# A spectral filter beside a gated feed-forward block on one core: the first three gated units split by row tile, the first loads reordered, two down projections put side by side, one pair of returns issued earlier

## The chip, the core and the metric

The kernel runs on one core of a Trainium2 chip. The metric is device time in microseconds (us) of one execution. The engines are named as in the profile: PE (TensorE matmul), PEld (its weight loads), DVE (VectorE), ACT (ScalarE), POOL (GpSimd) and SP (SyncE, which here only issues DMAs). ACT issues a few DMAs too; its issues are shown as ACTq, those of SP as SPq. Every engine works through its own list of instructions in order.

## The reference

For x of 2048 rows by 512 columns, with xn = layernorm(x) by row:

```python
def _A_ref(x, w_r, w_i):            # spectral filter
    X = rfft2(x.astype(float32)) * (w_r + 1j * w_i)     # 2048 x 257
    return irfft2(X, s=(S, D)).astype(bfloat16)

def _B_ref(x, w_gate, w_up, w_down):                    # 512 -> 1792 -> 512
    g = einsum("bsd,df->bsf", x, w_gate)
    u = einsum("bsd,df->bsf", x, w_up)
    return einsum("bsf,fd->bsd", gelu_tanh(g) * u, w_down)

out = x + _A_ref(xn, A_w_r, A_w_i) + _B_ref(xn, B_w_gate, B_w_up, B_w_down)
```

All inputs and the output are bf16.

## The kernel before

The rows form 16 tiles of 128 (x_sb, numbered j) and four blocks of four tiles (numbered b). The 1792 inner columns form 14 groups of 128 (numbered fc).

**Gated half.** A gated unit (`geglu_unit`, PE at L543) is one block and one group fc: four matmuls with the gate weights, four with the up weights, each for up to 512 rows, then a gelu on ACT (L555) and a product on DVE (L563) into hT. The gate and the up product take one PSUM bank each out of a ring, and the ring hands a bank out again only when ACT or DVE has read it. When a block's 14 units are done, four down units (`down_unit`, 14 matmuls at L589) project its hT by w_down, one per row tile, and DVE adds the result to x_sb (L600). The down units of blocks 0 to 2 have a ring of one bank, bank 7 (`ring_dn`); those of block 3 take the three banks of the gated units.

**Spectral half.** The Fourier transforms are chains of small matmuls: per row tile unit A (L616) and unit d (L642), a shuffle through device memory (`stage_p` out by SP, back into Tp by `shuffle`), per pair of frequency groups unit B (L691), the filter's product on DVE (L708 to L710) and unit c (L722), a second trip through device memory (`stage_g` out by SP, back into V by `back`, L739), and per row tile unit e (L753) and unit fin (L774), whose last steps run on ACT, DVE and POOL and add to x_sb. `back` is issued in four parts of two DMAs. Unit e of any tile waits for all eight (`perm2`).

**Order.** The program is one list per engine, written by hand (`_Sched`). Each entry carries the events that it waits for. Gated and down units serve as fillers between the spectral units: a list `fillers` holds the units of the four blocks in order, with the down units of block b-1 inserted among the gated units of block b at given places, and `filler(n)` takes the next n. One filler stands in each step of the A/d loop (16 steps), in steps 1 to 17 of the B/c loop (19 steps, numbered u), and in most steps of the e/fin loop. Between the B/c loop and the e/fin loop stand `todo["left"] - 15 - 3` fillers, five of them. For block 3 the insert places are (3, 5, 7, 14), so the five are the last gated unit of block 2, three gated units of block 3, and one down unit of block 2.

**Head.** SP issues the first loads, one stream (semaphore) for each x tile and one for each weight piece, gate and up together. DVE takes the row statistics (L411, L412), ACT the square root of the first two tiles (L417), DVE the reciprocal (L421) and the normalised rows (L434). For tiles 2 and 3 POOL computes the reciprocal root (L426, L427). In the meantime PE runs 46 and then 4 matmuls on zeros (`warm_up`, L524). Then PE transposes tiles 0 and 1 (`transposes_by_tile`, L447) into four banks, DVE and ACT copy them to xnT (L453, L455), and the first six gated units (`NHALF = 6`) run on rows 0 to 255 of block 0, then on rows 256 to 511, with a ring of six banks (`ring_first`). The transposes of tiles 2 and 3 (L473) stand behind the fourth of these units. The other eight groups of block 0 come as fillers of 512 rows.

Of the kernel before, what the change touches and what calls it, by code (L numbers as in the profile page):

```python
# [14 lines left out]
HD = 256  # L15
# [6 lines left out]
NFC = 14  # L22
NGG = 3
NX1 = 4
NWARM = (46, 4)
LN_EPS = 1e-5


# [199 lines left out]
def bass_parallel_sum__spectral_gfnet__glu_gated_geglu__prompt_kernel(  # L228
# [21 lines left out]
    with ExitStack() as es:  # L250
# [68 lines left out]
        def sp_bank_bf(slot):  # L319
# [8 lines left out]
        ring_tr = _Ring((3, 4), bank_readers)  # L328

        streams = [("pe", 1), ("act", 1), ("dve", 1), ("pool", 1)]  # L330
        streams += [(n, 16) for n in ("x0", "x1", "x2", "x3", "xc1", "xc2", "xc3", "ident", "small", "fa", "eg", "wd", "wr", "wi",
                                      "w0", "w1", "w2", "w3", "w4", "dr0", "dr1", "perm1", "jx0", "jx1", "jx2", "jx3", "vd0_0", "vd0_1", "vd0_2", "vd1_0", "vd1_1", "vd1_2", "vd2_0", "vd2_1", "vd2_2", "vd3_0", "vd3_1", "vd3_2", "perm2", "tr2", "tr3", "out")]
# [15 lines left out]
        def load_w(i, which=(0, 1), eng="sp"):  # L348
            a, b = WPIECES[i]
            for q in which:  # L350
                dst, src = ((wg_sb, B_w_gate), (wu_sb, B_w_up))[q]
                load("w%d" % i, dst[:, :, a:b], src[:, a:b].rearrange("(r p) f -> p r f", p=P), eng=eng)
            ev_w[i] = total("w%d" % i)

        def load_xc(m):
            ev = load("xc%d" % m, x_sb[:, 4 * m:4 * m + 4, :], xv[:, 4 * m:4 * m + 4, :])
# [1 line left out]
                ev_x[j] = ev  # L358

        ev_x = {}  # L360
        load_w(0, (1,), eng="act")
        for j in range(4):
            ev_x[j] = load("x%d" % j, x_sb[:, j, :], xv[:, j, :])
            if j == 1:
                load_w(0, (0,))
        load_w(1)
        load_w(2)
        load_xc(1)
        load_w(3)
# [66 lines left out]

        ev_xnT = {}

        def transposes_by_tile(a, b, ring):

            n = (b - a) * P
            slots = [ring.alloc(1) for _ in range(NDC)]
            banks = [sp_bank_bf(slot)[:, 0:n] for slot, _ in slots]
            evs = []
            for j in range(a, b):
                for r in range(NDC):
                    ev_t = sch.op("pe", lambda e, j=j, r=r: e.transpose(banks[r][:, (j - a) * P:(j - a + 1) * P], xn[:, j, r * P:(r + 1) * P], ident),  # L447
                                  deps=[ev_id, ev_xn[j]] + slots[r][1])
                    if j < b - 1:
                        continue  # L450
                    dst = xnT[:, r, a * P:b * P]
                    if r % 2 == 0:
                        ev = sch.op("dve", lambda e, dst=dst, r=r: e.tensor_copy(dst, banks[r]), deps=[ev_t])  # L453
                    else:
                        ev = sch.op("act", lambda e, dst=dst, r=r: e.activation(dst, banks[r], ACT.Copy), deps=[ev_t])  # L455
                    ring.add_reader(slots[r][0], ev)
                    evs.append(ev)
            for j in range(a, b):
                ev_xnT[j] = evs

        def transposes(a, b, ring, per=2):

# [66 lines left out]
        def geglu_unit(b, fc, a=0, w=512, ring=None):  # L529

            k = geg["k"]
            geg["k"] = k + 1
            s2 = k % NGG
            hb = b % 2
            ring = ring or ring_gu
            evw = [ev_w[i] for i, (lo, hi) in enumerate(WPIECES) if lo < (fc + 1) * P and fc * P < hi]
            evx = [ev_xnT[4 * b + i] for i in range(a // P, (a + w) // P)]
            gslot, gdeps = ring.alloc(1)

            def mm(e, wsb, slot, dcs=range(NDC)):  # L540
                ins = None
                for dc in dcs:
                    ins = e.matmul(gu_bank(slot)[:, 0:w], wsb[:, dc, fc * P:(fc + 1) * P], xnT[:, dc, b * 512 + a:b * 512 + a + w],  # L543
                                   start=(dc == 0), stop=(dc == NDC - 1))
                return ins

            if b == 0 and fc == 0 and a == 0:
                for dc in range(NDC):
                    ev_gm = sch.op("pe", lambda e, dc=dc: mm(e, wg_sb, gslot, (dc,)), deps=evw + [x[dc] for x in evx] + gdeps)
            else:  # L550
                ev_gm = sch.op("pe", lambda e: mm(e, wg_sb, gslot), deps=evw + evx + gdeps)
            uslot, udeps = ring.alloc(1)
            ev_um = sch.op("pe", lambda e: mm(e, wu_sb, uslot), deps=udeps)
            gg = gg_sb[s2][:, 0:w]
            ev_gg = sch.op("act", lambda e: e.activation(gg, gu_bank(gslot)[:, 0:w], ACT.Gelu_apprx_tanh),  # L555
                           deps=[ev_gm] + gg_readers[s2])
# [238 lines left out]
            finished(j, ev_o)  # L795


        NHALF = 6
        ln_stats(0)
        ln_stats(1)  # L800
        ev_sq = ln_sqrt(0, 2)
        sch.op("act", lambda e: e.activation(warm[:], eps_t[:], ACT.Gelu_apprx_tanh), deps=[ev_eps])
        ln_recip(0, 2, ev_sq)
        for n, ev in zip(NWARM, (None, ev_rstd[0])):
            warm_up(n, ev)
        ln_apply(0)
        ln_apply(1)
        transposes_by_tile(0, 2, ring_sp)
        ln_stats(2)
        ln_stats(3)  # L810
        ln_rstd(2, 4)
        for fc in range(NHALF):
            geglu_unit(0, fc, 0, 256, ring_first)
            if fc == 1:
                ln_apply(2)
                ln_apply(3)
                half_fold(0)
            if fc == 3:
# [141 lines left out]
```

## Time and profile before

| | us |
|---|---|
| median of three runs (180.42 to 181.10) | 181.07 |
| the profiled execution's own time | 180.17 |
| its span, first to last instruction | 178.4 |
| PE busy | 174.7 (98%) |
| DVE busy | 116.0 (65%) |
| ACT busy | 86.5 (49%) |
| POOL busy | 55.2 (31%) |
| first gated matmul starts | 7.14 |
| first unit e starts | 128.63 |

The share of PE counts the time in which any matmul is in flight. A matmul of 128x512 shows 0.38 us, while the next starts 0.216 us after it; so a late start is found by comparing starts, not by idle time alone. The granted clock of the profile's row is full throughout. Yet the 50 zero matmuls of 128 columns at the head fill the time from 0.97 to 6.22, 0.105 us each, while the eight transposes right behind them, of the same size, show 0.61 us together. The DMA engines are busy from 2 us on up to about 53 us, with the loads of weights, x, constants and filter.

### The profile page before, as it was taken

The page shows a single profiled execution, that of the slowest core. Times are in us where ns is not written, and L with a number is a line of the kernel's source. Part 1 is how long each engine was busy: PE and PEld are TensorE (multiplying, and loading weights), DVE is VectorE, ACT ScalarE, POOL GpSimd, SP SyncE. Part 2 cuts the span into 40 slices and gives each one's busy share as a digit, 9 for nine tenths or more (in the row PEclk, how much of TensorE's full clock was granted, in tenths as well). Part 3 has the DMA queues.
Part 4 walks back from the last instruction along what each step waited for, and adds up shares of the span by engine and source line. Part 5 has one row for each costly group of instructions (what it writes and reads, how often), then busy time and mean ns, then how long its engine had stood idle before and what let it go on. Part 6 is the DMA issues. An engine that isn't in the chain of part 4 may idle for free.

```text
span 178.4 us, 3133 instructions
## 1 busy us (share of the span) xinstructions
PE 174.7 (98%) x1136; PEld 98.2 (55%) x1136; DVE 116.0 (65%) x250; ACT 86.5 (49%) x159; POOL 55.2 (31%) x54
## 2 busy tenths in 40 slices
PE   7999999999999999999999999999999999999994
PEld 7888465555555544454555555444455555555443
DVE  3768958798685628438586785954355868885731
ACT  2644357777362633066375764632173536662100
POOL 0073290373630000000000000000017869997760
PEclk9999999999999999999999999999999999999999
DMA  4999999999998693913435666744500111111101
GB/s 147 323 342 379 372 379 149 202 156 239 221 159 198 150 313 106 324 53 81 123 104 125 123 184 149 177 90 117 118 6 29 59 59 32 61 65 48 41 29 59
DMA packets 37520, 27.15 MB, mean 152 GB/s; under 512 B 6656, under 2 KB 36736, under 8 KB 37376
## 3 DMA queue, kind: packets, MB, share of 16 engines
q1 hardware_dynamic: 33664, 24.95, 55.1%
q10 hardware_dynamic: 3840, 2.00, 5.8%
q8 instruction: 9, 0.15, 0.4%
q14 instruction: 7, 0.06, 0.2%
HBM read 17.48 MB, written 6.30 MB: 133 GB/s over the span
## 4 chain that ended last, share of the span: by engine, by line
PE 87%; POOL 5%; DVE 5%; issue 1%
PE ps L543 48%; PE ps L589 25%; POOL bufC L504 5%; PE ps L524 3%; PE ps L722 2%; PE ps L753 2%; PE ps L774 2%; PE ps L691 2%; DVE bufA L434 2%; DVE hT L563 1%; PE ps L616 1%; PE ps L642 1%; PE ps L473 1%; DVE bufB L509 1%; POOL rstd L427 1%
## 5 line engine op out<-in xcount | busy, mean ns | idle before, releaser
L543 PE MATMUL ps<-xnT,wg_sb 128*128 128x512 bf16 (+1 forms) x248 | 58.5, 359 | 0.3 <-DVE xnT L453 0.3
L543 PE MATMUL ps<-xnT,wu_sb 128*128 128x512 bf16 (+1 forms) x248 | 58.6, 359 | 0.0
L563 DVE TENSOR_TENSOR hT<-ps,gg 128x512 bf16<-128x512 f32 (+1 forms) x62 | 39.3, 637 | 23.2 <-PE ps L543 21.6
L589 PE MATMUL ps<-wd_sb,hT 128*128 128x512 bf16 (+2 forms) x238 | 50.7, 367 | 0.0
L555 ACT ACTIVATE gg<-ps 128x512 bf16<-128x512 f32 (+1 forms) x62 | 34.4, 555 | 25.2 <-PE ps L543 23.6
L788 POOL TENSOR_TENSOR bufC<-bufC 128x256 bf16<-128x256 f32 x16 | 14.7, 919 | 86.5 <-DVE bufC L785 86.5
L543 PEld LDWEIGHTS ps<-xnT,wu_sb 128*128 128x128 bf16 x248 | 24.2, 98 | 24.2
L589 PEld LDWEIGHTS ps<-wd_sb,hT 128*128 128x128 bf16 x238 | 22.4, 98 | 23.2
L543 PEld LDWEIGHTS ps<-xnT,wg_sb 128*128 128x128 bf16 x248 | 23.0, 98 | 15.4 <-issue 0.5
L600 DVE TENSOR_TENSOR x_sb<-ps,x_sb 128x512 bf16<-128x512 f32 (+2 forms) x17 | 11.2, 660 | 23.9 <-PE ps L589 23.9
L792 POOL TENSOR_TENSOR x_sb<-x_sb,bufC 128x512 bf16<-128x512 bf16 x16 | 18.7, 1169 | 2.3
L504 POOL TENSOR_TENSOR bufC<-bufA 128x1024 bf16<-128x1024 bf16 x8 | 16.8, 2124 | 7.9 <-DVE bufA L434 7.9
L758 ACT ACTIVATE bufA<-ps 128x512 bf16<-128x512 f32 x16 | 9.4, 597 | 16.9 <-PE ps L753 16.9
L727 ACT ACTIVATE Vp<-ps 128x514 bf16<-128x514 f32 x16 | 9.5, 599 | 15.4 <-PE ps L722 15.4
L650 ACT ACTIVATE bufB<-ps 128x512 bf16<-128x512 f32 x16 | 11.9, 743 | 9.5 <-PE ps L642 9.5
L411 DVE BATCH_NORM_STATS2 st<-x_sb 128x6 f32<-128x512 bf16 x16 | 10.9, 678 | 2.2 <-DMA x_sb<-in_A_x_dram 2.2
L784 DVE TENSOR_TENSOR bufC<-bufC,ps 128x256 f32<-128x256 f32 x16 | 6.7, 421 | 5.3 <-ACT bufC L781 5.3
L696 ACT ACTIVATE Xc<-ps 128x514 bf16<-128x514 f32 x12 | 7.0, 595 | 1.0 <-PE ps L691 1.0
L623 ACT ACTIVATE tmp<-ps 128x512 bf16<-128x512 f32 x9 | 5.4, 597 | 4.4 <-PE ps L616 4.4
L426 POOL TENSOR_SCALAR rstd<-ag 128x4 f32<-128x4 f32 (+1 forms) x4 | 1.3, 316 | 19.9 <-DVE ag L412 19.9
L781 ACT ACTIVATE bufC<-ps 128x256 f32<-128x256 f32 x16 | 6.0, 378 | 2.6 <-PE ps L774 2.6
L788 DVE TENSOR_TENSOR bufC<-bufC 128x256 bf16<-128x256 f32 x16 | 6.8, 425 | 0.5
(50 smaller groups left out, 138.0 us busy)
## 6 DMA issues: line engine op xcount, KB each, us to landing
stage_g<-Vp SPq DMA_DIRECT2D x16, 128.5 KB, 3.1
bufC<-stage_p SPq DMA_DIRECT2D x4, 512.0 KB, 5.5
out_dram<-x_sb SPq DMA_DIRECT2D x15, 128.0 KB, 1.8
wd_sb<-in_B_w_down_dram SPq DMA_DIRECT2D x1, 1792.0 KB, 14.8
stage_p<-bufB SPq DMA_DIRECT2D x7, 256.0 KB, 5.6
wr_sb<-in_A_w_r_dram SPq DMA_DIRECT2D x6, 257.0 KB, 10.8
wi_sb<-in_A_w_i_dram SPq DMA_DIRECT2D x6, 257.0 KB, 10.0
JX<-Xc SPq DMA_DIRECT2D x24, 64.2 KB, 2.3
```

Source lines behind the costliest of these rows:

```text
L411: ev = sch.op("dve", lambda e: e.bn_stats(st[:, j, :], x_sb[:, j, :]), deps=[ev_x[j]])
L504: ev_hf[m] = [sch.op("pool", lambda e, t=t, op=op: e.tensor_tensor(half[:, m, t, :, :], rows[:, 0, :, :], rows[:, 1, :, :], op), deps=deps ...
L543: ins = e.matmul(gu_bank(slot)[:, 0:w], wsb[:, dc, fc * P:(fc + 1) * P], xnT[:, dc, b * 512 + a:b * 512 + a + w], start=(dc == 0), stop=(d ...
L555: ev_gg = sch.op("act", lambda e: e.activation(gg, gu_bank(gslot)[:, 0:w], ACT.Gelu_apprx_tanh), deps=[ev_gm] + gg_readers[s2])
L563: ev_h = sch.op("dve", lambda e: e.tensor_tensor(hT[hb][:, fc, a:a + w], gu_bank(uslot)[:, 0:w], gg, ALU.mult), deps=[ev_um, ev_gg] + hdeps)
L589: ins = e.matmul(bank(slot)[:, 0:w], hT[hb][:, fc, jj * P:(jj + 1) * P], wd_sb[:, fc, cs], start=(fc == 0), stop=(fc == NFC - 1))
L600: ev_a = sch.op("dve", lambda e, slot=slot, cs=cs, w=w: e.tensor_tensor(x_sb[:, j, cs], bank(slot)[:, 0:w], x_sb[:, j, cs], ALU.add), deps ...
L650: ev_T[j] = sch.op("act", lambda e: e.activation(dst, src, ACT.Copy), deps=[ev_p])
L727: ev_v = sch.op("act", lambda e: e.activation(Vp[sv][:], sp_pair(slot), ACT.Copy), deps=[ev_p] + Vp_readers[sv])
L758: ev_ZT[j] = sch.op("act", lambda e: e.activation(ZT[:, :, j, :], src, ACT.Copy), deps=[ev_p] + [ev_xnT[i][0] for i in (11, 15)])
L788: y = [sch.op(("dve", "pool")[h], lambda e, h=h, op=op: e.tensor_tensor(rS[s2][:, h * HD:(h + 1) * HD], yeS[s2][:, 0, :], yeS[s2][:, 1, :] ...
L792: ev_o = sch.op("pool", lambda e: e.tensor_tensor(x_sb[:, j, :], x_sb[:, j, :], rS[s2], ALU.add), deps=[a, b, ev_xn[j]] + ev_acc.get(j, []))
```

## The change

Five things change.

- The weight streams are split: gate and up of each piece have a semaphore each, and a unit's up matmuls wait for the up load on their own.
- The first loads on SP come in the order x0, x1, gate 0, gate 1, x2, up 1, x3, then piece 2 as before (up 0 stays on ACT). Before it was x0, x1, gate 0, x2, x3, gate 1, up 1.
- The head works by row tile. Square root and reciprocal are done for tile 0 and tile 1 apart; `transpose_first` transposes one tile into two banks, and DVE copies tile 0, ACT copies tile 1. The first three groups run on the 128 rows of tile 0, then on those of tile 1, and groups 3 to 6 on 256 rows. `NHALF` is 7, so that seven groups are run in two halves and seven are left as fillers. The transposes of tiles 2 and 3 stand behind group 5. The zero matmuls are 42 and 3.
- The insert places of block 3 are (3, 3, 7, 14), and the fillers before the e/fin loop are `todo["left"] - 15 - 2`. These are again five: three gated units of block 3 and two down units of block 2, one right behind the other. The last gated unit of block 2 now falls to step 17 of the B/c loop.
- Both returns of the third part are issued by ACT at the head of step 17; they stood at the ends of steps 17 and 18. The returns of parts one and two keep their places on ACT.

```diff
-NWARM = (46, 4)
+NWARM = (42, 3)
...
-            ev_w[i] = total("w%d" % i)
+                name = "w%d%s" % (i, "gu"[q])
+                load(name, dst[:, :, a:b], src[:, a:b].rearrange("(r p) f -> p r f", p=P), eng=eng)
+                ev_w[i, q] = total(name)
...
         load_w(0, (1,), eng="act")
-        for j in range(4):
-            ev_x[j] = load("x%d" % j, x_sb[:, j, :], xv[:, j, :])
-            if j == 1:
-                load_w(0, (0,))
-        load_w(1)
+        load_x(0)
+        load_x(1)
+        load_w(0, (0,))
+        for q in range(2):
+            load_w(1, (q,))
+            load_x(2 + q)
         load_w(2)
...
+        def transpose_first(j, eng):
+            evs = []
+            for h in range(2):
+                slot, bdeps = ring_tr.alloc(1)
+                bank = sp_bank_bf(slot)[:, 0:HD].rearrange("p (r s) -> p r s", r=2)
+                def f_tr(e, h=h, bank=bank):
+                    ins = None
+                    for r in range(2):
+                        ins = e.transpose(bank[:, r, :], xn[:, j, (2 * h + r) * P:(2 * h + r + 1) * P], ident)
+                    return ins
+                ev_t = sch.op("pe", f_tr, deps=[ev_id, ev_xn[j]] + bdeps)
+                dst, src = xnT[:, 2 * h:2 * h + 2, j * P:(j + 1) * P], bank
+                if eng == "dve":
+                    ev = sch.op("dve", lambda e, dst=dst, src=src: e.tensor_copy(dst, src), deps=[ev_t])
+                else:
+                    ev = sch.op("act", lambda e, dst=dst, src=src: e.activation(dst, src, ACT.Copy), deps=[ev_t])
+                ring_tr.add_reader(slot, ev)
+                evs += [ev, ev]
+            ev_xnT[j] = evs
...
-            ev_um = sch.op("pe", lambda e: mm(e, wu_sb, uslot), deps=udeps)
+            ev_um = sch.op("pe", lambda e: mm(e, wu_sb, uslot), deps=evw_up + udeps)
...
-        NHALF = 6
+        NQUARTER, NHALF = 3, 7
         ln_stats(0)
         ln_stats(1)
-        ev_sq = ln_sqrt(0, 2)
+        ev_sq = [ln_sqrt(j, j + 1) for j in range(2)]
         sch.op("act", lambda e: e.activation(warm[:], eps_t[:], ACT.Gelu_apprx_tanh), deps=[ev_eps])
-        ln_recip(0, 2, ev_sq)
+        ln_recip(0, 1, ev_sq[0])
         for n, ev in zip(NWARM, (None, ev_rstd[0])):
             warm_up(n, ev)
         ln_apply(0)
+        ln_recip(1, 2, ev_sq[1])
+        transpose_first(0, "dve")
         ln_apply(1)
-        transposes_by_tile(0, 2, ring_sp)
+        for fc in range(NQUARTER):
+            geglu_unit(0, fc, 0, P, ring_first)
+            if fc == 0:
+                transpose_first(1, "act")
         ln_stats(2)
-        ln_stats(3)
+        for fc in range(NQUARTER):
+            geglu_unit(0, fc, P, P, ring_first)
+            if fc == 0:
+                ln_stats(3)
         ln_rstd(2, 4)
-        for fc in range(NHALF):
+        for fc in range(NQUARTER, NHALF):
             geglu_unit(0, fc, 0, 256, ring_first)
-            if fc == 1:
+            if fc == NQUARTER:
                 ln_apply(2)
                 ln_apply(3)
                 half_fold(0)
-            if fc == 3:
+            if fc == NHALF - 2:
                 transposes(2, 4, ring_tr)
...
-                for n, at in enumerate((4, 7, 10, 13) if b < 3 else (3, 5, 7, 14)):
+                for n, at in enumerate((4, 7, 10, 13) if b < 3 else (3, 3, 7, 14)):
                     units.insert(at + n, ("d", b - 1, n))
...
         for u in range(19):
+            for pq in {10: (0,), 11: (1,), 14: (0,), 15: (1,), 17: (0, 1)}.get(u, ()):
+                back((u - 9) // 4 if u < 17 else 2, pq, "act")
...
-            if u in (9, 10, 13, 14, 17, 18):
-                back(u // 4 - 2, (u - 9) % 4, "act")
         for pq in range(2):
             back(3, pq, "sp")
-        filler(todo["left"] - 15 - 3)
+        filler(todo["left"] - 15 - 2)
```

More of the change, by code (lines that the diff above doesn't have):

```diff
@@ L330, in bass_parallel_sum__spectral_gfnet__glu_gated_geglu__prompt_kernel @@
         streams = [("pe", 1), ("act", 1), ("dve", 1), ("pool", 1)]
+        streams += [("w%d%s" % (i, q), 16) for i in range(5) for q in "gu"]
         streams += [(n, 16) for n in ("x0", "x1", "x2", "x3", "xc1", "xc2", "xc3", "ident", "small", "fa", "eg", "wd", "wr", "wi",
-                                      "w0", "w1", "w2", "w3", "w4", "dr0", "dr1", "perm1", "jx0", "jx1", "jx2", "jx3", "vd0_0", "vd0_1", "vd0_2", "vd1_0", "vd1_1", "vd1_2", "vd2_0", "vd2_1", "vd2_2", "vd3_0", "vd3_1", "vd3_2", "perm2", "tr2", "tr3", "out")]
+                                      "dr0", "dr1", "perm1", "jx0", "jx1", "jx2", "jx3", "vd0_0", "vd0_1", "vd0_2", "vd1_0", "vd1_1", "vd1_2", "vd2_0", "vd2_1", "vd2_2", "vd3_0", "vd3_1", "vd3_2", "perm2", "tr2", "tr3", "out")]
         for name, inc in streams:
@@ L351, in load_w @@
                 dst, src = ((wg_sb, B_w_gate), (wu_sb, B_w_up))[q]
-                load("w%d" % i, dst[:, :, a:b], src[:, a:b].rearrange("(r p) f -> p r f", p=P), eng=eng)
-            ev_w[i] = total("w%d" % i)
+                name = "w%d%s" % (i, "gu"[q])
+                load(name, dst[:, :, a:b], src[:, a:b].rearrange("(r p) f -> p r f", p=P), eng=eng)
+                ev_w[i, q] = total(name)
         def load_xc(m):
@@ L360, in bass_parallel_sum__spectral_gfnet__glu_gated_geglu__prompt_kernel, with load_x @@
         ev_x = {}
+        def load_x(j):
+            ev_x[j] = load("x%d" % j, x_sb[:, j, :], xv[:, j, :])
         load_w(0, (1,), eng="act")
-        for j in range(4):
-            ev_x[j] = load("x%d" % j, x_sb[:, j, :], xv[:, j, :])
-            if j == 1:
-                load_w(0, (0,))
-        load_w(1)
+        load_x(0)
[4 more added lines that the diff above has]
+            load_x(2 + q)
         load_w(2)
@@ L437, in bass_parallel_sum__spectral_gfnet__glu_gated_geglu__prompt_kernel @@
         ev_xnT = {}
[L439 to L443, printed above, removed]
+        def transpose_first(j, eng):
             evs = []
[L445 to L459, printed above, removed]
+            for h in range(2):
[15 more added lines that the diff above has]
+            ev_xnT[j] = evs
         def transposes(a, b, ring, per=2):
@@ L535, in geglu_unit @@
             ring = ring or ring_gu
-            evw = [ev_w[i] for i, (lo, hi) in enumerate(WPIECES) if lo < (fc + 1) * P and fc * P < hi]
+            pieces = [i for i, (lo, hi) in enumerate(WPIECES) if lo < (fc + 1) * P and fc * P < hi]
+            evw, evw_up = ([ev_w[i, q] for i in pieces] for q in range(2))
             evx = [ev_xnT[4 * b + i] for i in range(a // P, (a + w) // P)]
```

## The prediction

> **What bounds the kernel now.** I read the page first, for the engines' shares:
>
> ```profile
> span 178.4 us, 3133 instructions
> PE 174.7 (98%) x1136; PEld 98.2 (55%) x1136; DVE 116.0 (65%) x250; ACT 86.5 (49%) x159; POOL 55.2 (31%) x54
> ```
>
> PE is in flight nearly all the time. The change alters no matmul's work except at the warm-up, so it can gain only by starting PE's real work sooner and by removing late starts of matmuls; it loses by adding such starts. The chain of waits (start, length, what) shows where they are:
>
> ```profile
> 6.70 0.30 DVE xnT L453
> 7.00 0.14 issue
> 7.14 3.67 PE ps L543 x32
> ...
> 53.36 0.04 issue
> 53.40 0.40 PE ps L616 x4
> ...
> 125.56 3.02 PE ps L589 x14
> 128.58 0.04 issue
> 128.63 0.62 PE ps L753 x8
> ```
>
> The first gated matmul starts at 7.14. Later PE is late at two places of this chain that matter here: unit A at 53.40, behind a DVE/POOL chain of normalising and folding, and the first unit e at 128.63, behind the returns. A start tells more than the idle time: 512-column matmuls start 0.216 apart, so the up matmuls that began at 52.30 would have let A start at 53.16 (0.24 lost), and the 14 of the down unit that began at 125.39 would have let e start at 128.41 (0.22 lost).
>
> The timeline of the head (start, length, instruction) shows what sets 7.14, and how tiles 2 and 3 come in:
>
> ```profile
> 3.98 0.66 DVE L411 BATCH_NORM_STATS2 st<-x_sb 128x6 f32<-128x512 bf16 x1
> 4.67 0.18 DVE L412 BATCH_NORM_AGGREGATE ag<-st 128x2 f32<-128x6 f32 x1
> 5.42 0.73 DVE L434 TENSOR_SCALAR bufA<-x_sb,ag,rstd 128x512 bf16<-128x512 bf16 x2
> 6.22 0.61 PE L447 MATMUL ps<-small,bufA 128*128 128x128 bf16 x8
> 8.62 0.18 DVE L412 BATCH_NORM_AGGREGATE ag<-st 128x2 f32<-128x6 f32 x1
> 8.89 0.23 POOL L426 TENSOR_SCALAR rstd<-ag 128x2 f32<-128x2 f32 x1 [8.04 <-DVE ag L412]
> 9.20 0.73 POOL L427 TENSOR_TENSOR rstd<-rstd,half_t 128x2 f32<-128x2 f32 x1
> 10.76 0.62 PE L473 MATMUL ps<-small,bufA 128*128 128x128 bf16 x8
> 11.42 0.60 ACT L482 ACTIVATE xnT<-ps 128x512 bf16<-128x512 bf16 x1 [0.63 <-PE ps L473]
> ```
>
> Statistics, root, normalising, transposes, copy and a first matmul follow each other. The warm-up ends just as the second tile is normalised.
>
> **The head, walked.** Statistics are unchanged, to 4.85. The root of tile 0 no longer waits for tile 1's, so the reciprocal runs at 4.85 and tile 0 is normalised at 5.06 to 5.47 (reciprocal to normalising took 0.21 before, one normalising 0.41). PE cannot take it yet: 45 zero matmuls at 0.106 end at 5.74. So the removed five, not the earlier root, set the transposes. Before, the first copy started 0.48 after the first transpose and the first gated matmul 0.44 after that; now the copy starts at 6.20 (two transposes instead of five, but at the slow pace) and the matmul at 6.64. Its gate weights were issued at 1.64 and landed 4.8 later, at 6.44: just in time, still third on SP. The second copy starts 0.22 after the first, so the gate's last two matmuls go at 6.88, and tile 0's first unit is through at 7.16.
>
> I take 128-column matmuls at 0.056 (the transposes behind the warm-up, each with weights of its own), so four need 0.22. Tile 1's transposes end at 7.38 (normalised by 7.05, behind the copies on DVE), two more units of tile 0 end at 8.27, ACT's copies of tile 1 by 8.18, and three units of tile 1 end at 9.60. Before, the same work (three units at 0.874 from 7.14) ended at 9.76. So the earlier start is worth 0.16 only.
>
> Then the order on DVE takes it back. The products of 128 columns have one near row, the last 128-column add of L600 at 0.29; gelu I estimate at 0.27, continuing its 0.60 and 0.38 for 512 and 256 columns. The statistics of tile 2 now stand behind tile 0's three products. Gelu 2 and 3 stand behind ACT's two copies, so the third product runs at 8.59; tile 2's statistics follow at 8.81 (x2 lands near 7.7, x3 near 9.0, by the landings of the same bytes before), a product at 9.63, tile 3's statistics from 9.84 to 10.75. They ended at 8.80 before. POOL's two operations and the waits between need 1.13 (8.80 to 9.93), two normalisings 0.74: 12.66. PE reaches the transposes of tiles 2 and 3 at 12.32, after groups 3 to 5, and after 0.10 lost in group 4, whose up bank waits for a product behind tile 3's statistics. They start at 12.70 (0.38 lost), and only one unit (0.87) covers the copies instead of two: the second half starts at 14.06. Before it started at 12.97 with one unit less, so 13.84 is the like time. The head loses 0.22. Bounds: without these stalls it gains 0.28; with DVE's chain 0.4 later it loses 0.6. I keep 0.22, as each duration comes from a near row.
>
> [...] The eight transposes and the groups of four in units A and e run at 56 ns; a run of 24 narrow gated matmuls is not shown before.
>
> [...]
>
> **The middle.** One gated unit goes from the fillers into the head, so each filler place holds the next unit, and every spectral step comes 1.73 later against the same remaining work. Between the normalising that starts the chain to 53.40 and that unit A now stand two down units instead of one, 1.29 more cover: the 0.24 goes. Between the last unit d and the first unit B the cover shrinks by 1.29, to 11.87. The shuffled data came 11.77 after that unit d (63.57 to 75.34); that chain should shorten, since the last write no longer queues beside the first shuffle. I cost it at 0; without that, up to 0.2. The other waits keep a down unit in each four steps: 0.
>
> **The returns.** ACT reaches the head of step 17 behind a copy of `Vp` and waits for the third part's writes (the fourth of them landed 4.6 after its unit c, 110.84 to 115.43). Behind it on ACT is only step 17's copy, and a down unit of 3.02, which needs no ACT, covers the wait: 0. Without the cover it would be 1.6. The second return then leaves before the last two writes instead of between them.
>
> **The two down units.** They share bank 7, so the second waits for DVE's add of the first. The timeline of a later down unit gives the price:
>
> ```profile
> 133.43 3.18 PE L589 MATMUL ps<-wd_sb,hT 128*128 128x512 bf16 x14
> 136.45 0.39 PE L753 MATMUL ps<-fa,bufB 128*128 128x128 bf16 x4
> 136.65 0.69 DVE L600 TENSOR_TENSOR x_sb<-ps,x_sb 128x512 bf16<-128x512 f32 x1 [1.13 <-PE ps L589]
> ```
>
> PE went on at 136.45. Had it needed the bank, it would have waited for the add's end at 137.34 and 0.04 to 0.14 more (the two "issue" rows above): 0.93 to 1.03 lost, I take 0.98. All matmuls behind it are delayed, and no DVE work covers it. The five fillers last 3 x 1.73 + 2 x 3.02 + 0.98 = 12.2 instead of 9.93, so the 0.22 at the first unit e goes.
>
> **The end.** Two down units instead of three stand behind the last unit fin. POOL ended its last add 5.55 after PE was through with fin (172.58 against 167.03), and the two last down units give 6.05; the add of the first 384 columns comes 0.05 late, at most 0.1.
>
> **Sum.** 0.22 - 0.24 + 0.98 - 0.22 + 0.05 = +0.8. Against the profiled execution's own 180.17 that is 181.0; its median run was 181.07, 0.90 longer, so I predict 181.9.
>
> **Rivals.**
> - Not slower: the timed runs wait longer for the returns than the profile does. That the data landed within 0.22 of need is chance; stage_g writes took from 2.3 to 4.9. If the whole 0.90 between profile and median is this wait, the change removes 1.1 instead of 0.22 and ends at 181.0. It decides once the wait exceeds about 1.0. For it: the gap itself; against: the gap has other possible places.
> - Slower: the DVE order at the head costs more, 0.6, and the shuffle's cover fails by 0.2: 182.5. For it: tile 3's statistics wait for everything ahead on DVE.
> - Slower: narrow gated matmuls don't keep 56 ns. Between the fast row and the zero matmuls' 0.106, 48 of them cost 0 to 2.4; half of it gives 183.1. Against: weights change with every transpose too.
> - The change doesn't stall at the two down units: then 180.9. Against: one bank in the ring.
>
> **Chances.** As summed 0.58, with 0.25 of it above 182.0; returns' wait 0.17; head 0.13; narrow matmuls 0.04; no stall or another gain 0.08. 0.5%, 0.9 us, is about what a measurement can tell from no change. Slower by more: 0.25 + 0.12 + 0.04 = 0.41; faster by more: 0.12, from the second, the last and luck; the rest, 0.47, within. The range runs from 180.6 (returns' wait with a head without stalls) to 182.8 (head at its bound and an add of 1.03), leaving out 183.1.
>
> **What would show it.** A first gated matmul near 6.6; transposes of tiles 2 and 3 near 12.7, waiting for DVE; a pause of some 1.0 between two groups of 14 at L589 near 129; no wait of L753 for a DMA. I am wrong if the pause is absent, or if the head comes out far from +0.2.

## The result: slower by 1.0%, and the profile after

| | before | after |
|---|---|---|
| median, both on one chip (us) | 180.84 (180.42 to 181.10) | 182.64 (182.39 to 183.00) |
| ratio to before, 95% interval | | 1.0103 [1.0074, 1.0132] |
| profiled execution, its span | 180.17, 178.4 | 182.57, 180.8 |
| PE's last matmul starts | 175.91 | 176.63 |
| from there to the end of the span | 2.49 | 4.17 |

The forecast was 181.9, with a range from 180.6 to 182.8. The time lies in it, but 0.74 above the forecast. As an effect, +0.8 was forecast, and the medians of this table differ by 1.80. The last two rows say where the error is: of the 2.4 us that the profiled span has grown, 0.72 come before PE's last matmul and 1.7 behind it. The forecast had put 0.74 before it and 0.05 behind it.

First the page of the kernel after, its span and its engines:

```profile
span 180.8 us, 3208 instructions
PE 174.6 (97%) x1163; PEld 99.1 (55%) x1163; DVE 116.0 (64%) x255; ACT 87.4 (48%) x164; POOL 55.2 (31%) x54
```

The busy times are those of before, within 1 us on every engine. So what was added is waiting. The page's part 4 says on whom, by the engines' shares of the chain that ended last:

```profile
PE 73%; POOL 13%; DVE 5%; issue 3%; DMA 3%; POOLq 1%; ACT 1%; SPq 0%; DVEq 0%
```

The same line of the page before:

```profile
PE 87%; POOL 5%; DVE 5%; issue 1%
```

POOL holds 13% of the chain; before, it held 5%. The chain of waits itself (start, length, what) runs through PE until 144.7, and from 146.7 through POOL, with DVE between POOL's steps from 164 on:

```profile
1.65 4.99 DMA wg_sb<-in_B_w_gate_dram
...
125.54 3.04 PE ps L598 x14
129.35 3.19 PE ps L598 x14
...
141.68 3.04 PE ps L598 x14
...
146.70 0.97 POOL bufC L797
...
174.39 1.40 POOL x_sb L801
```

In the new line numbers L552 is the gated unit (L543 before), L598 the down unit, L609 its add to x_sb, L762 unit e, L783 unit fin, L793, L794 and L797 fin's steps on DVE, and POOL's are a second L797 and the add to x_sb, L801.

**The head.** The timeline of the kernel after (start, length, instruction, idle time before it and what ended it):

```profile
6.68 0.48 PE L552 MATMUL ps<-xnT,wg_sb 128*128 128x128 bf16 x4 [0.30 <-DMA wg_sb<-in_B_w_gate_dram]
7.45 0.39 PE L552 MATMUL ps<-xnT,wg_sb 128*128 128x128 bf16 x4
9.23 0.39 PE L552 MATMUL ps<-xnT,wg_sb 128*128 128x128 bf16 x4
9.91 0.68 DVE L418 BATCH_NORM_STATS2 st<-x_sb 128x6 f32<-128x512 bf16 x1
10.73 0.80 DVE L572 TENSOR_TENSOR hT<-ps,gg 128x128 bf16<-128x128 f32 x3
11.98 0.73 DVE L441 TENSOR_SCALAR bufA<-x_sb,ag,rstd 128x512 bf16<-128x512 bf16 x2 [0.45 <-POOL rstd L434]
12.77 0.62 PE L481 MATMUL ps<-small,bufA 128*128 128x128 bf16 x8 [0.23 <-DVE bufA L441]
14.17 0.60 PE L552 MATMUL ps<-xnT,wg_sb 128*128 128x256 bf16 x4
```

The first gated matmul comes at 6.68, the transposes of tiles 2 and 3 at 12.77, waiting for DVE. By the distance of the starts they are 0.39 late. The second half starts at 14.17, against a like time of 13.84: the head loses 0.33 in this pair of profiles. Heads vary from one execution to the next: in the six profiles here that have the head of after unaltered, the second half starts between 14.03 and 14.43, and in the four with the head of before the like time lies between 13.84 and 14.19. Steadier is the distance from the first gated matmul to the second half, 7.40 to 7.49 with the new head and 6.70 (once 6.88) with the old one. From 7.45 to 9.23 lie eight groups of four matmuls, 1.78 us, so 0.0556 for one.

**The two down units**, in the timeline:

```profile
125.38 3.19 PE L598 MATMUL ps<-wd_sb,hT 128*128 128x512 bf16 x14
128.60 0.69 DVE L609 TENSOR_TENSOR x_sb<-ps,x_sb 128x512 bf16<-128x512 f32 x1 [2.33 <-PE ps L598]
129.35 3.19 PE L598 MATMUL ps<-wd_sb,hT 128*128 128x512 bf16 x14 [0.79 <-DVE x_sb L609]
132.38 0.61 PE L762 MATMUL ps<-fa,bufB 128*128 128x128 bf16 x8
```

The last matmul of the first unit starts at 128.18, so the second could have started at 128.40; it starts at 129.35, 0.95 late. Unit e waits for no DMA now. The wait of unit A that stood at 53.40 is gone as well, and so is one of 0.1 in front of a unit c, which before started at 102.86.

**The end**, in the timeline from the unit fin of tile 11 on:

```profile
164.28 0.69 DVE L609 TENSOR_TENSOR x_sb<-ps,x_sb 128x512 bf16<-128x512 f32 x1 [1.98 <-POOL x_sb L801]
164.88 0.41 DVE L793 TENSOR_TENSOR bufC<-bufC,ps 128x256 f32<-128x256 f32 x1
165.21 0.41 DVE L794 TENSOR_TENSOR bufC<-bufC,ps 128x256 f32<-128x256 f32 x1
165.70 0.96 POOL L797 TENSOR_TENSOR bufC<-bufC 128x256 bf16<-128x256 f32 x1 [1.53 <-DVE bufC L794]
166.81 1.15 POOL L801 TENSOR_TENSOR x_sb<-x_sb,bufC 128x512 bf16<-128x512 bf16 x1
168.06 0.69 DVE L609 TENSOR_TENSOR x_sb<-ps,x_sb 128x512 bf16<-128x512 f32 x1 [1.98 <-POOL x_sb L801]
...
170.61 6.24 PE L598 MATMUL ps<-wd_sb,hT 128*128 128x512 bf16 x42
171.85 0.69 DVE L609 TENSOR_TENSOR x_sb<-ps,x_sb 128x512 bf16<-128x512 f32 x1 [1.98 <-POOL x_sb L801]
...
176.62 1.15 POOL L801 TENSOR_TENSOR x_sb<-x_sb,bufC 128x512 bf16<-128x512 bf16 x1
177.87 0.76 DVE L609 TENSOR_TENSOR x_sb<-ps,x_sb 128x384 bf16<-128x384 f32 x2 [1.29 <-POOL x_sb L801]
```

Before, the same adds on DVE waited for PE:

```profile
166.62 0.69 DVE L600 TENSOR_TENSOR x_sb<-ps,x_sb 128x512 bf16<-128x512 f32 x1 [1.13 <-PE ps L589]
166.87 9.26 PE L589 MATMUL ps<-wd_sb,hT 128*128 128x512 bf16 x56
...
171.43 1.15 POOL L792 TENSOR_TENSOR x_sb<-x_sb,bufC 128x512 bf16<-128x512 bf16 x1
...
175.38 0.56 DVE L600 TENSOR_TENSOR x_sb<-ps,x_sb 128x384 bf16<-128x384 f32 x1 [1.58 <-PE ps L589]
176.17 0.29 DVE L600 TENSOR_TENSOR x_sb<-ps,x_sb 128x128 bf16<-128x128 f32 x1 [0.22 <-PE ps L589]
```

In a step of the e/fin loop that has a down unit, PE needs 8 matmuls of 0.056 and 14 of 0.216, 3.47. In after, the down unit of tile 11 stands in the step of tile 11's own fin, that of tile 12 in the step of tile 12's, that of tile 13 likewise. Its add (L609) goes into the same rows of x_sb as POOL's last step of fin (L801), and it waits for that (1.98). DVE works through its list in order, so the next fin's steps (L793, L794) stand behind this add (they start 0.60 and 0.93 after it), and POOL waits for them (1.53). The ring is closed: POOL's two steps, the add, DVE's two steps, and again. The fence shows one turn, 164.28 to 168.06: 3.78 us, more than PE's 3.47. So POOL falls behind PE, ends its last add at 177.77 instead of 172.58, and the last two adds of DVE run together behind it.

### The profile page after: what moved, and what is told of

Read it like the earlier page. It is cut to its first block, busy times and chain, and to the rows that moved or that the text cites. A ratio compares the mean times of both kernels' runs of the same rounds, so it can differ in the third digit from the quotient of the medians.

```text
span 180.8 us, 3208 instructions
## 1 busy us (share of the span) xinstructions
PE 174.6 (97%) x1163; PEld 99.1 (55%) x1163; DVE 116.0 (64%) x255; ACT 87.4 (48%) x164; POOL 55.2 (31%) x54
## 4 chain that ended last, share of the span: by engine, by line
PE 73%; POOL 13%; DVE 5%; issue 3%; DMA 3%; POOLq 1%; ACT 1%; SPq 0%; DVEq 0%
PE ps L552 44%; PE ps L598 18%; POOL x_sb L801 7%; POOL bufC L797 5%; DMA wg_sb<-in_B_w_gate_dram 3%; PE ps L731 2%; PE ps L651 2%; PE ps L625 2%; PE ps L700 2%; DVE x_sb L609 1%; DVE bufC L794 1%; DVE bufC L793 1%; PE ps L481 1%; PE ps L762 1%; DVE st L418 1%
## 5 line engine op out<-in xcount | busy, mean ns | idle before, releaser
L552 PE MATMUL ps<-xnT,wg_sb 128*128 128x512 bf16 (+2 forms) x264 | 59.3, 347 | 0.3 <-DMA wg_sb<-in_B_w_gate_dram 0.3
L552 PE MATMUL ps<-xnT,wu_sb 128*128 128x512 bf16 (+2 forms) x264 | 59.2, 347 | 0.0
L572 DVE TENSOR_TENSOR hT<-ps,gg 128x512 bf16<-128x512 f32 (+2 forms) x66 | 39.5, 606 | 24.3 <-PE ps L552 22.1
L598 PE MATMUL ps<-wd_sb,hT 128*128 128x512 bf16 (+2 forms) x238 | 50.8, 366 | 0.8 <-DVE x_sb L609 0.8
L564 ACT ACTIVATE gg<-ps 128x512 bf16<-128x512 f32 (+2 forms) x66 | 35.1, 532 | 22.8 <-PE ps L552 19.8
L797 POOL TENSOR_TENSOR bufC<-bufC 128x256 bf16<-128x256 f32 x16 | 14.7, 920 | 89.5 <-DVE bufC L794 89.5
L552 PEld LDWEIGHTS ps<-xnT,wu_sb 128*128 128x128 bf16 x264 | 24.9, 98 | 23.9 <-DVE hT L572 0.2
L598 PEld LDWEIGHTS ps<-wd_sb,hT 128*128 128x128 bf16 x238 | 22.3, 98 | 24.3 <-DVE x_sb L609 1.3
L552 PEld LDWEIGHTS ps<-xnT,wg_sb 128*128 128x128 bf16 x264 | 23.8, 98 | 15.1 <-DMA wg_sb<-in_B_w_gate_dram 0.6
L609 DVE TENSOR_TENSOR x_sb<-ps,x_sb 128x512 bf16<-128x512 f32 (+2 forms) x17 | 11.1, 660 | 26.6 <-PE ps L598 18.2
L801 POOL TENSOR_TENSOR x_sb<-x_sb,bufC 128x512 bf16<-128x512 bf16 x16 | 18.7, 1169 | 2.3
L793 DVE TENSOR_TENSOR bufC<-bufC,ps 128x256 f32<-128x256 f32 x16 | 6.7, 419 | 4.5 <-ACT bufC L790 4.5
L797 DVE TENSOR_TENSOR bufC<-bufC 128x256 bf16<-128x256 f32 x16 | 6.8, 424 | 0.5
```

The source lines that it names most:

```text
L598: ins = e.matmul(bank(slot)[:, 0:w], hT[hb][:, fc, jj * P:(jj + 1) * P], wd_sb[:, fc, cs], start=(fc == 0), stop=(fc == NFC - 1))
L609: ev_a = sch.op("dve", lambda e, slot=slot, cs=cs, w=w: e.tensor_tensor(x_sb[:, j, cs], bank(slot)[:, 0:w], x_sb[:, j, cs], ALU.add), deps ...
L797: y = [sch.op(("dve", "pool")[h], lambda e, h=h, op=op: e.tensor_tensor(rS[s2][:, h * HD:(h + 1) * HD], yeS[s2][:, 0, :], yeS[s2][:, 1, :] ...
L801: ev_o = sch.op("pool", lambda e: e.tensor_tensor(x_sb[:, j, :], x_sb[:, j, :], rS[s2], ALU.add), deps=[a, b, ev_xn[j]] + ev_acc.get(j, []))
```

## The experiments

All kernels here compute the whole result. The two terms that were right in size (the head and the two down units) and the one that was not (the end) are separate questions. For the end, the wait of L609 for POOL was seen; open was what brings it about: the later start of unit e (132.38 against 128.63) with all that follows it on DVE and POOL, or the place of the last down units alone. Each run lists its distance from PE's last matmul to the end of the span, which is 2.49 in before and 4.17 in after.

**1. Filler ahead of fin.** In after, the filler of each step of the e/fin loop is put ahead of unit fin, so that the add of a down unit stands ahead of the same tile's fin:

```diff
-            if j >= 2:
-                unit_fin(j - 2)
             if 1 <= j < NJ:
                 filler()
+            if j >= 2:
+                unit_fin(j - 2)
```

> The changed kernel with one edit: in the e/fin loop the filler stands ahead of unit fin instead of behind it, so a down unit's add is queued on DVE ahead of the fin of its own tile and waits for no POOL add. Theory A (the late end comes from DVE adds of tiles 11 to 13 waiting for POOL's add of the same tile, and POOL then waiting for DVE): the three waits of 1.98 before L609 go, POOL's three waits of 1.53 fall to about 1.2, the span falls from 180.8 to about 179.4 (POOL starts at 136.7 and needs 39.6 as before the change, to 176.3). Theory B (POOL alone is too slow for the time left behind the first unit e, whatever waits for it): the span stays above 180.4.

Measured 182.79, ratio 1.0139 [1.0097, 1.0181], span 180.9. The waits did change in the loop: the adds wait for PE, and POOL 1.21 instead of 1.53:

```profile
166.52 0.69 DVE L609 TENSOR_TENSOR x_sb<-ps,x_sb 128x512 bf16<-128x512 f32 x1 [1.62 <-PE ps L598]
...
171.46 0.97 POOL L797 TENSOR_TENSOR bufC<-bufC 128x256 bf16<-128x256 f32 x1 [1.21 <-DVE bufC L794]
...
178.03 0.76 DVE L609 TENSOR_TENSOR x_sb<-ps,x_sb 128x384 bf16<-128x384 f32 x2 [1.28 <-POOL x_sb L801]
```

But every fin comes a filler later: POOL begins its first at 138.03 instead of 136.71, and the last three stand together at 169.8, where POOL needs 2.2 for each, up to 177.93. The end is POOL's again, 4.42 behind PE, and the span of 179.4 that was expected of the ring is missed. The edit took one cause away and set another in its place, so it settles nothing about the first.

**2. Another bank.** In after, the second of the two down units takes a bank of the gated units' ring:

```diff
-            ring, bank = (ring_gu if b == 3 else ring_dn), bank_of
+            ring, bank = (ring_gu if b == 3 or (b, jj) == (2, 1) else ring_dn), bank_of
```

> The changed kernel with one edit: the second of the two adjacent down units (block 2, tile 9) takes a bank of the gated units' ring instead of bank 7, so it need not wait for the add of the first. Theory A (everything behind the first unit e hangs on its start, through POOL): the 0.95 between the two down units goes, the first unit e starts 0.95 earlier, at 131.4, and the whole 0.95 shows in the span: 179.85. Theory C (the end is set by something that doesn't hang on that start, so the 0.95 is covered): the span stays at 180.6 to 180.9.

Measured 181.52, ratio 1.0069 [1.0047, 1.0091], span 179.7. The pause is gone: the matmuls of both units stand in one row (26 of the 28; two records are missing), and unit e starts at 131.30, 1.08 earlier.

```profile
125.69 5.78 PE L598 MATMUL ps<-wd_sb,hT 128*128 128x512 bf16 x26
131.30 0.61 PE L762 MATMUL ps<-fa,bufB 128*128 128x128 bf16 x8
```

PE's last matmul starts 1.08 earlier too (of this, 0.95 are the pause, and 0.12 come from the head, whose second half starts at 14.05 in this execution), the span is 1.1 shorter, and 4.15 still lie behind PE. So the shared bank costs its 0.95 in PE's list, the profiled span shows all of it, and it has no part in the 1.7 at the end. The ratios to before fall by less, from 1.0103 to 1.0069, some 0.6 us, and their intervals touch: of the timed runs no more than the direction is shown.

**3. The old insert places.** In after, (3, 5, 7, 14) for block 3:

```diff
-for n, at in enumerate((4, 7, 10, 13) if b < 3 else (3, 3, 7, 14)):
+for n, at in enumerate((4, 7, 10, 13) if b < 3 else (3, 5, 7, 14)):
```

> The changed kernel with the insert places of block 3 as before, (3, 5, 7, 14); the five fillers ahead of the e/fin loop are then four gated units and one down unit. The last three down units still stand in the steps of their own tiles' fin. Theory A (the late start of unit e is what makes POOL the bound): unit e starts near 130.1, POOL begins near 134.5 and ends near 175.6, about as PE needs it; span 178.2 to 178.7, that is 2.1 to 2.6 less than the changed kernel. Theory D (the down units' places beside their own fin cost a fixed 1.7 at the end): PE's last matmul near 175.7, span 179.8.

Measured 181.52, ratio 1.0070 [1.0048, 1.0091], span 179.8, last matmul of PE at 175.69 and 4.1 behind it. No two down units stand together, unit e starts at 130.15, and the end is as long as in after.

**4. One filler more ahead of unit e, in the kernel before.** Nothing else of the change:

```diff
-        filler(todo["left"] - 15 - 3)
+        filler(todo["left"] - 15 - 2)
```

> The kernel before with six fillers ahead of the e/fin loop instead of five, so that the last three down units stand in the steps of their own tiles' fin, as in the changed kernel, and two down units are left at the end. The wait for the returns at the first unit e (0.21) goes. Theory A: unit e starts 1.5 later than before, at 130.1, POOL begins near 134.5 and ends near 175.6; the end is that of the kernel before within 0.4 (span 178.0 to 178.8). Theory D (the places alone cost 1.7): span 179.8 to 180.1.

Measured 181.69, ratio 1.0084 [1.0054, 1.0114], span 180.1. PE's last matmul starts at 175.92, as in before (175.91), and 4.18 lie behind it. The timeline of this kernel shows the ring with the numbers of after:

```profile
163.56 0.69 DVE L600 TENSOR_TENSOR x_sb<-ps,x_sb 128x512 bf16<-128x512 f32 x1 [1.98 <-POOL x_sb L792]
164.99 0.97 POOL L788 TENSOR_TENSOR bufC<-bufC 128x256 bf16<-128x256 f32 x1 [1.53 <-DVE bufC L785]
...
167.36 0.69 DVE L600 TENSOR_TENSOR x_sb<-ps,x_sb 128x512 bf16<-128x512 f32 x1 [1.98 <-POOL x_sb L792]
```

One number, the count of fillers ahead of the loop, makes the whole 1.7, without the head, the places or the returns of the change. It both starts unit e later and moves the down units by a step, so this run alone doesn't say which of the two it is. If POOL were short of time behind unit e, the end would follow the time from the first unit e to PE's last matmul, which is 47.28 in before. It does not: with 45.54 in the runs 3 and 4, and 44.25 in run 2 and in after, the end is 4.1 to 4.2 in all four. Run 7 (44.25) and run 9 (45.55) keep these times and place the last down units otherwise, and in both PE ends the chain again. Together they settle it: it is the places.

**5. The returns alone.** In before, only the third part's returns go to the head of step 17:

```diff
         for u in range(19):
+            for pq in {10: (0,), 11: (1,), 14: (0,), 15: (1,), 17: (0, 1)}.get(u, ()):
+                back((u - 9) // 4 if u < 17 else 2, pq, "act")
...
-            if u in (9, 10, 13, 14, 17, 18):
-                back(u // 4 - 2, (u - 9) % 4, "act")
```

> The kernel before with only the returns of the third part moved to the head of step 17. My reading: ACT's wait for the writes lies beside work of PE that needs no ACT, so the time stays within 0.3 of the kernel before; at best the 0.21 in front of the first unit e goes. Rival: the return blocks ACT's copies and PE's unit c is late, 0.5 or more slower.

Measured 180.21 against 180.66, ratio 0.9975 [0.9955, 0.9994]. The same kernel, measured again:

> The kernel before with only the returns of the third part moved, once more and in more rounds: the earlier run gave 0.9975 of the kernel before. If the 0.2 in front of the first unit e is the gain, the ratio lies at 0.997 to 1.000 and the first unit e waits for no transfer; if the earlier ratio was chance, 0.999 to 1.002.

Measured 180.26 against 180.22, ratio 1.0006 [0.9990, 1.0022]. The first result is not confirmed; the move has no effect that these runs can show. Unit e waits for no DMA in either. The view of waits of the second run shows the wait that ACT took over, which costs nothing:

```profile
ACT Vp L727 <- DMA stage_g<-Vp: 1.5, 1, 1.5
```

**6. The statistics earlier.** In after, tile 2's statistics stand on DVE behind tile 0's first product, and tile 3's behind its third:

```diff
                 transpose_first(1, "act")
-        ln_stats(2)
+                ln_stats(2)
+        ln_stats(3)
         for fc in range(NQUARTER):
             geglu_unit(0, fc, P, P, ring_first)
-            if fc == 0:
-                ln_stats(3)
```

> The changed kernel with the statistics of tile 2 queued on DVE behind the first product of tile 0 and those of tile 3 behind the third, instead of behind the third of tile 0 and the first of tile 1. If the order on DVE is what holds the transposes of tiles 2 and 3 (0.39 late), they start at about 12.35 instead of 12.77 and the span falls by 0.3 to 0.45, to 180.4. If not (products of 128 columns come too late and the gated units wait for banks instead), the span stays within 0.15 of 180.8.

Measured 182.51, ratio 1.0107 [1.0076, 1.0138], span 180.7. In its timeline the transposes no longer wait for DVE, but two gated groups wait for a bank instead:

```profile
9.12 0.23 PEld L552 LDWEIGHTS ps<-xnT,wu_sb 128*128 128x128 bf16 x4 [0.18 <-DVE hT L572]
9.81 0.60 PE L552 MATMUL ps<-xnT,wg_sb 128*128 128x256 bf16 x4
10.09 0.67 DVE L572 TENSOR_TENSOR hT<-ps,gg 128x128 bf16<-128x128 f32 x3
10.51 0.60 PE L552 MATMUL ps<-xnT,wu_sb 128*128 128x256 bf16 x4
12.69 0.61 PE L481 MATMUL ps<-small,bufA 128*128 128x128 bf16 x8
```

The up matmuls at 9.13 are 0.17 late, and those at 10.51 are 0.26 late (256 columns start 0.109 apart, so four from 9.81 end at 10.25). Together 0.43, where 0.39 and, at group 4, 0.05 were lost before the transposes in after. The first of the two waits names DVE's product; the second names none, and starts 0.15 behind the end of the first of the three products that begin at 10.09. From the first gated matmul to the second half it is 7.36, against 7.40 to 7.49 with the old order: the gain in the head is 0.04 to 0.13. What the statistics leave to the products, the products then lack. That it is DVE's amount of work in these 5 us, whatever its order, is the likely reading; two orders alone don't show it.

**7. The order of the last down units.** In after, those of block 3 run in the order of tiles 14, 15, 12, 13, so that tiles 12 and 13 have their fin two steps behind them. The split add goes to the last one, tile 13, and the first one, tile 14, is the one that takes its last two groups on their own:

```diff
-            for h, cs in enumerate((slice(0, 384), slice(384, D)) if j == NJ - 1 else (slice(0, D),)):
+            for h, cs in enumerate((slice(0, 384), slice(384, D)) if j == NJ - 3 else (slice(0, D),)):
...
-                if b == 3 and jj == 0:
+                if b == 3 and jj == 2:
...
-        fillers += [("d", 3, n) for n in range(4)]
+        fillers += [("d", 3, n) for n in (2, 3, 0, 1)]
```

> The changed kernel with block 3's down units in the order of tiles 14, 15, 12, 13 (the last one split in 384 and 128 columns as before). Tiles 14 and 15 are then projected ahead of their own fin, and tiles 12 and 13 long after theirs, so that of the last three down units in the e/fin loop only tile 11's add still waits for POOL's add of the same step. First unit e and its distance to PE's end are unchanged. Theory A2 (the loss at the end is DVE, in order, held by adds that wait for POOL, with the next fin queued behind them): the end is PE's again, span 179.0 to 179.3. Theory B (POOL is short of time behind the first unit e, whatever waits): span 180.3 or more.

Measured 181.71, ratio 1.0058 [1.0040, 1.0077], span 179.9. Only tile 11's wait for POOL is left:

```profile
164.53 0.69 DVE L609 TENSOR_TENSOR x_sb<-ps,x_sb 128x512 bf16<-128x512 f32 x1 [1.99 <-POOL x_sb L801]
167.15 0.69 DVE L609 TENSOR_TENSOR x_sb<-ps,x_sb 128x512 bf16<-128x512 f32 x1 [0.80 <-PE ps L598]
...
177.14 0.29 DVE L609 TENSOR_TENSOR x_sb<-ps,x_sb 128x128 bf16<-128x128 f32 x1 [0.23 <-PE ps L598]
```

The last add is PE's again, at 177.14. The span missed what was expected of it for two other reasons: in this execution x landed later (the first statistics waited 3.0 for it, 2.2 in after), and the first gated matmul started at 7.03 instead of 6.68; and four results leave at the end one behind the other on SP (issued at 176.60, 176.98, 177.45 and 177.94), so that 3.02 lie behind PE's last matmul instead of 2.5. The six timed runs all lie between 181.48 and 181.87; whether x landed late in the others too is open.

**8. Four fillers.** In after, the old places and one filler less ahead of unit e:

```diff
-... else (3, 3, 7, 14)):
+... else (3, 5, 7, 14)):
...
-        filler(todo["left"] - 15 - 2)
+        filler(todo["left"] - 15 - 3)
```

> The changed kernel with the insert places of block 3 as before, (3, 5, 7, 14), and four fillers ahead of the e/fin loop instead of five (three gated units, one down unit); the last down units then stand one step behind their own tile's fin and three are left at the end, as before the change. The four last 8.2 behind the last unit c, the returns need some 8.8, so the first unit e waits about 0.5 at 128.9. If the late end of the changed kernel is all in its two adjacent down units and in the places of the last ones, this comes to a span of 178.4 to 178.9, level with the kernel before; if the new head or the returns hold more of it, 179.3 or more.

Measured 180.97, ratio 1.0021 [0.9998, 1.0044], span 179.2. The end is back to 2.45. But with four fillers instead of five there is too little work ahead of unit e:

```profile
129.47 0.62 PE L762 MATMUL ps<-fa,bufB 128*128 128x128 bf16 x8 [0.77 <-DMA bufB<-stage_g]
```

By the distance of the starts unit e is 0.94 late for the returns, more than the 0.5 that the expectation allowed.

**9. The lag restored.** In after, the old places, five fillers ahead of unit e, none in step 1, that of step 2 ahead of its fin, and the statistics as in 6. Three down units stand behind the last fin again:

```diff
-... else (3, 3, 7, 14)):
+... else (3, 5, 7, 14)):
...
             if j < NJ:
                 unit_e(j)
+            if j == 2:
+                filler()
             if j >= 2:
                 unit_fin(j - 2)
-            if 1 <= j < NJ:
+            if 3 <= j < NJ:
                 filler()
```

> The changed kernel with three edits: the insert places of block 3 as before, (3, 5, 7, 14), so that no two down units of block 2 are adjacent; no filler in step 1 of the e/fin loop and the one of step 2 ahead of its fin, so that five fillers still stand ahead of the first unit e but each of the last down units falls one step behind its own tile's fin, and three are left at the end; and the earlier statistics of the run before. If the late end is all in the adjacent down units and in the places of the last ones, PE's last matmul starts near 175.6 and the span ends 2.45 behind it as before the change: 177.9 to 178.3, level with the kernel before or up to 0.3 less. If the places are not the reason, the end stays 4.1 behind PE's last matmul: 179.7.

Measured 179.61 against 180.22, ratio 0.9968 [0.9957, 0.9980], span 177.7: faster than after, and 0.3% faster than before. This small gain was measured once, and run 5 shows that a first result of this size can fail to come again. Its timeline has the adds waiting for PE, as before the change:

```profile
166.02 0.69 DVE L609 TENSOR_TENSOR x_sb<-ps,x_sb 128x512 bf16<-128x512 f32 x1 [1.13 <-PE ps L598]
...
175.56 0.29 DVE L609 TENSOR_TENSOR x_sb<-ps,x_sb 128x128 bf16<-128x128 f32 x1 [0.22 <-PE ps L598]
```

PE's last matmul starts at 175.31, 0.60 before that of before; 2.4 lie behind it. Unit A, the unit c of 102.86 and unit e wait for nothing (0.24, 0.1 and 0.21 in before), and the head is even: the second half starts at 13.81, against the like time of 13.84. So what the change gains is about 0.6 us in this pair of profiles, and nearly all of it lies in the waits of the middle, not in the head that it was mostly about. The even head is mostly this execution's own: its first gated matmul starts 0.21 earlier than in after (last section), while its distance from there to the second half is 7.34, as in run 6.

## Why the prediction was right and where it was wrong

- **The head, walked.** Right in its waits, a little low: 0.22 forecast, 0.33 measured in the pair of profiles, which other executions move by some tenths. The first gated matmul 6.64 against 6.68 (there by chance in part: it waited for its gate weights, which landed at 6.63 and not at 6.44), the transposes 12.70 against 12.77 and 0.38 against 0.39 late, the bank of group 4 0.10 against 0.05, the second half 14.06 against 14.17. The forecast blamed the order on DVE; in run 6 another order gains next to nothing, so the order alone is not the cause.
- **128 columns at 0.056.** Right: 0.0556. The eight groups of four from 7.45 to 9.23 took 1.78, with a weight load for each matmul; at the 0.106 of the zero matmuls they would have taken an estimated 3.4. So the rival of narrow matmuls falls.
- **The middle.** Right: unit A's 0.24 is gone, and the shuffle made no new wait. The 0.1 in front of a unit c, which also went, was not in the sum.
- **The returns.** Right at 0: unit e waits for no DMA. ACT's wait for the writes shows in run 5 (1.5), where it costs nothing; in after the view of waits has none. The rival that timed executions wait longer for the returns than the profile put 0.9 on this; in run 5, where the profile's wait is gone by the move alone, the kernel is as fast as before (1.0006 when measured again; a gain of 0.9 would be 0.995, outside both intervals). So the rival falls.
- **The two down units.** Right: 0.98 forecast, 0.95 measured, and run 2 shows the shared bank as its cause. The rival without a stall falls; the 0.22 won at unit e was 0.21.
- **The end.** This step failed: 0.05, at most 0.1, was forecast, 1.7 measured. It took POOL's 5.55 from the end of fin to its last add out of the trace of before and set it beside the 6.05 of two down units. But the 5.55 was not POOL's own work: it held only as long as the adds stood one step behind the fin of their tile. The forecast moved the down units by a step, counted what they are to PE, and did not follow their adds on DVE: whom they wait for there (POOL's add to the same rows) and who stands behind them (the next fin). Counted from the first down matmul behind the last fin (166.87 and 170.61) to the end of POOL's last add (172.58 and 177.77), 5.71 became 7.16, which is more than the 6.05 of cover. Counted from the same matmuls, POOL's adds to tiles 12, 13 and 14 start 0.33, 0.64 and 1.45 later than before: two turns of the ring, each 0.3 longer than PE's step, and a third of 3.80, where POOL's adds to tiles 13 and 14 lay 2.99 apart before. The last add of 128 columns, which in before started 0.26 behind PE's last matmul, now stands as the second of a row from 177.87, 1.7 behind it. None of the rivals named it.
- **From the profile to the median.** The forecast added the 0.90 by which the median of before lay above its profiled execution. After the change the two lie 0.07 apart, so this term was 0.83 too high, and hid half of the error at the end: the terms are +1.63 (end), -0.83 (this one) and -0.02 (all before PE's last matmul), 0.78 in all between the time and the forecast's 181.86 before rounding. The 0.90 was no property of the kernel: in three later series its median was 180.12 (14 runs), 180.66 (21) and 180.22 (23), that is 0.05 below to 0.49 above the profiled 180.17. What moves it from series to series stays open.
- **The range.** That the time lies in it is luck. With the end as measured and all else as forecast, the sum gives 183.5, which is outside. The upper bound of 182.8 is also more than the parts that it names: the head at 0.6 and an add of 1.03 make 182.3, and the time lies in the half microsecond between.

## What to carry to other kernels

When an instruction group is moved in a hand-written order, follow all its parts, on every engine: the add that ends a group may land behind a writer of the same rows on another engine, and in front of work that this writer's engine needs. A distance read from a trace ("POOL ends 5.55 after PE") is only a constant if the order that made it stays; and where two engines hand rows to and fro, compare one turn of that ring with the step of the engine that bounds the kernel. Look also for two groups that share one accumulator bank and are put side by side: here the second waited for the first one's reader, which cost 0.95.

## What the runs showed of the hardware that was not expected

The pace of the matmuls at the head changed in one execution earlier than in another, with the same instructions on PE up to there. The first transposes of after, and those of run 9:

```profile
5.75 0.63 PE L456 MATMUL ps<-small,bufA 128*128 128x128 bf16 x4
```

```profile
5.73 0.39 PE L456 MATMUL ps<-small,bufA 128*128 128x128 bf16 x4
```

Four matmuls take 0.63 in the one and 0.39 in the other, though the matmuls on zeros began at 0.97 in both and the transposes at 5.75 and 5.73. The granted clock of the profiles reads full (1.0) in both. In both the first gated matmul then waited for its gate weights, whose landing moved too (6.63 and 6.41). The first gated matmul of an unchanged head also varied, from 7.14 (before) to 7.38 (run 4). What sets the moment at which the pace changes no run here shows. So a few tenths at the head of one profile are no evidence; distances inside one trace are steadier: from the first gated matmul to the second half it is 7.40 to 7.49 in the six profiles with the head of after, whose second halves start up to 0.40 apart.
